# A planned attention and gated-FFN kernel: first transpose in two steps, first weights in halves, burst rules by stage

## The chip, the cores and the metric

The kernel runs on one core of a Trainium2 chip. Its time is the device time of that core in microseconds (us). Six runs of the kernel before are given; the profile comes from one further execution.

## What is computed

Attention with a squared ReLU in place of a softmax, over 8 batches of 12 heads, 448 positions and 64 values a head; then a gated feed-forward network (FFN) over the 3,584 tokens (768 values each, 1,536 inside):

```python
scores = scale * np.matmul(q, k.transpose(0, 1, 3, 2))
attn = np.maximum(scores, 0.0) ** 2 / S
attn_out = np.matmul(attn, v)
x = attn_out.transpose(0, 2, 1, 3).reshape(B * S, H * D)
out = (np.maximum(x @ w_gate, 0.0) * (x @ w_val)) @ w_out
```

## The kernel before

**Work.** The heads are taken in quads: three groups of four heads per batch. A quad goes through these steps. Its queries and keys are brought into a transposed layout `qkT`. A *score step* (`Attention.s`, L622) multiplies four 64x64 corners of the TensorE array at a time and leaves scores in a pair of PSUM banks. A ReLU takes them to SBUF (`at`; ACT at L631 or DVE at L633), a square follows in place (ACT L643 or DVE L645), and a *PV* (`Attention.pv`, L661, 28 matmuls) multiplies by V; its result is copied to `xT` (L676 on ACT). A quad of batches 1 to 7 has seven score steps of four matmuls with 448 columns.

Batch 0 is cut in two so that it can start early: first the 192 query columns (`HALF`) that are loaded first, with all keys, then the 256 late columns. Its quads are transposed on TensorE by `transpose_first` (L494, then L501 for the late queries), those of batch 1 by `transpose_pe` (L527), and all later ones by a copy on DVE (`perm`, L550) and two DMA transposes from the SP queue (L556).

The FFN of batches 0 and 1 is plain (`gv_plain`, L721, twelve blocks of 128 columns, for batch 0 partly with 192 and 256 tokens). The later pairs of batches use a Strassen scheme with seven products (`gv_strassen`, L821), and so does the output product of every pair (`out_both`, L936). Their sums and differences run on DVE.

**Order.** `plan` is a list scheduler that runs while the program is built. Every operation is an `Op` with a cost on each engine that may do it, its inputs, and the buffers that it takes and frees. The planner keeps a clock for each engine, picks the operation that can start first, and emits all operations by their planned start. Each engine then runs its own list in that order; semaphores make it wait where the plan was too early. TensorE has two lists, `att` (attention) and `ffn`. In the opening (`first`) it takes the transposes, batch 0's first scores and its PVs. After that it mixes the lists: `debt` counts FFN time since the last attention step, and when it passes `START` or `LATEST` times the share due, a *burst* of attention steps is taken, up to the next step marked `cut` (`CUTS` says after which steps). Where a gap of TensorE is planned before 21 us (`FILL_UNTIL`), `filler` puts matmuls into it (L1065) that nobody reads; they read a constant tile and write a spare bank.

**Loads.** All loads go out from the POOL queue (L394), in the order of the string `ORDER`: after queries and keys of batch 0, `V` is V of batch 0, `L` its late queries, a digit a weight chunk of 256 columns (gate and value), a letter `abcxyz` a quad of batches 1 and 2, `opqr` the four parts of `w_out`. `raw` has one buffer, so a later quad's load waits for the `perm` of the one before.

```python
    ORDER = 'VL102acbx34y5zroqp'
...
        op = pe(emit, 1.35 if g == 0 else 1.05, deps=st.qk_ops + [id_op], alloc=[ps2, st.qt_buf])
...
    first, att = [list(trans), first, att], []
```

## Time and profile before

| | us |
|---|---|
| median of six runs | 412.49 |
| lowest and highest | 410.02, 415.91 |
| the six | 410.02, 410.5, 415.3, 415.91, 410.35, 414.48 |
| the profiled execution | 409.13 |
| its span | 407.3 |
| matmuls for scores, L622 (756) | 49.9 busy |
| matmuls for PV with `vv`, L661 (700 of 756) | 33.7 busy |
| DMA transposes, issue to landing, median | 6.8 |

The rows name an engine (PE is TensorE's matmuls, PEld its weight loads, DVE VectorE, ACT ScalarE, POOL and SP the two queues that issue DMAs), a line of the kernel, output and input, and how many. "Busy" adds up the durations of single instructions; matmuls overlap each other in the array, so TensorE's busy time has to be read together with what it was busy with. A wait is idle time of an engine just before an instruction, with what ended it. A window such as 60.00:100.00 is a stretch of the span in us.

### The profile page before, as it was taken

Reading aid. Unit: us, or ns where it says so; the run is one execution under the profiler, and the core shown is the slowest. Engines: PE = TensorE matmul, PEld = TensorE weight load, DVE = VectorE, ACT = ScalarE, POOL = GpSimd, SP = SyncE. Lnnn points to the kernel's source line nnn. Section 1 sums busy time; section 2 is a strip of 40 time slices with the busy share of each in tenths; the row PEclk is TensorE's granted clock in tenths of the full one; section 3 lists DMA queues with packets and bytes.
Section 4 is the critical chain, followed back from the end, with each engine's and each line's share of the span. In section 5 each row is a group of like instructions: output and inputs, shape, how many; then the busy total and the mean of one; then the engine's idle time right before and its main releaser. Section 6 shows DMA issues by size and latency. Waiting matters only on the chain.

```text
span 407.3 us, 8787 instructions
## 1 busy us (share of the span) xinstructions
PE 398.3 (98%) x3481; PEld 207.6 (51%) x3481; DVE 324.3 (80%) x573; ACT 257.0 (63%) x385; POOL 74.2 (18%) x119
## 2 busy tenths in 40 slices
PE   8979999999999999999999999999999999999995
PEld 4567654444445544444445544444455555555562
DVE  2777999997899889897798699888798746766652
ACT  2888888556776677888486489756574544434221
POOL 8737215201222112222110122110000000000000
PEclk9999999999999999999999999999999999999999
DMA  8999999988869999885669699750003340000144
GB/s 122 189 199 202 172 177 135 202 123 113 115 89 186 171 167 116 113 94 84 76 78 180 134 183 119 101 69 1 2 0 79 98 98 2 1 0 2 42 106 124
DMA packets 75736, 43.43 MB, mean 107 GB/s; under 512 B 37808, under 2 KB 75696, under 8 KB 75696
## 3 DMA queue, kind: packets, MB, share of 16 engines
q0 software_dynamic: 33328, 23.60, 43.1%
q1 hardware_dynamic: 42208, 19.08, 27.5%
q8 instruction: 27, 0.44, 0.5%
q10 hardware_dynamic: 160, 0.20, 0.1%
q14 instruction: 13, 0.11, 0.1%
HBM read 47.19 MB, written 11.01 MB: 143 GB/s over the span
## 4 chain that ended last, share of the span: by engine, by line
PE 92%; DMA 3%; DVE 3%; ACT 1%; issue 1%; SPq 0%; DVEq 0%
PE ps L821 34%; PE ps L936 23%; PE ps L721 13%; PE ps L622 9%; PE ps L661 8%; PE ps L1065 3%; DMA qkT<-perm 2%; DVE at L633 1%; PE ps L494 1%; DVE at L645 1%; PE ps L527 1%; DMA out_dram<-o 1%; DVE hT L731 0%; SPq L556 0%; ACT xT L676 0%
## 5 line engine op out<-in xcount | busy, mean ns | idle before, releaser
L631 ACT ACTIVATE at<-ps 128x896 bf16<-128x896 f32 (+3 forms) x111 | 97.4, 911 | 20.9 <-PE ps L622 20.7
L770 ACT COPY f<-ps 128x448 f32<-128x448 f32 x99 | 51.8, 532 | 47.0 <-PE ps L821 45.6
L633 DVE TENSOR_SCALAR at<-ps 128x896 bf16<-128x896 f32 (+4 forms) x60 | 63.0, 1052 | 13.3 <-PE ps L622 12.7
L645 DVE TENSOR_TENSOR at<-at 128x896 bf16<-128x896 bf16 (+4 forms) x118 | 69.5, 611 | 3.7 <-ACT at L631 3.3
L821 PE MATMUL ps<-xT,gvT 128*128 128x448 bf16 x216 | 52.6, 353 | 0.0
L643 ACT ACTIVATE at<-at 128x896 bf16<-128x896 bf16 (+4 forms) x53 | 49.8, 940 | 4.1 <-DVE at L633 3.4
L821 PE MATMUL ps<-sx,wv 128*128 128x448 bf16 x216 | 52.2, 353 | 0.0
L821 PE MATMUL ps<-xT,wg 128*128 128x448 bf16 x216 | 51.6, 353 | 0.0
L622 PE MATMUL ps<-qkT 64*64 64x448 bf16 (+2 forms) x756 | 49.9, 341 | 0.5 <-DMA qkT<-perm 0.2
L821 PEld LDWEIGHTS <-gvT 128*128 128x128 bf16 x324 | 30.4, 98 | 32.0 <-issue 5.4
L936 PE MATMUL ps<-wo,hT 128*128 128x384 bf16 x240 | 43.8, 326 | 0.1
L936 PEld LDWEIGHTS <-hT 128*128 128x128 bf16 x312 | 29.7, 98 | 22.9 <-issue 3.9
L394 POOL DMA_DIRECT2D vv<-in_v_dram x44 | 26.7, 620 | 78.1 <-PE ps L622 77.5
L936 PEld LDWEIGHTS <-sh 128*128 128x128 bf16 x288 | 27.0, 98 | 21.3 <-issue 3.7
L772 ACT ACTIVATE f<-ps 128x384 f32<-128x384 f32 x39 | 19.0, 491 | 28.6 <-PE ps L936 28.6
L661 PE MATMUL ps<-at,vv 64*64 64x448 bf16 (+2 forms) x700 | 33.7, 329 | 0.0
L721 PE MATMUL ps<-xT,wv 128*128 128x448 bf16 (+2 forms) x180 | 32.2, 315 | 0.8 <-DVE at L633 0.8
L721 PE MATMUL ps<-xT,wg 128*128 128x448 bf16 (+2 forms) x180 | 32.4, 316 | 0.3 <-ACT xT L676 0.3
L861 DVE TENSOR_TENSOR hT<-ps,g 128x448 bf16<-128x448 f32 x36 | 22.4, 622 | 12.1 <-PE ps L821 12.0
L394 POOL DMA_DIRECT2D raw<-in_k_dram x18 | 11.3, 628 | 112.5 <-DVE perm L550 93.7
L676 ACT CAST xT<-ps 128x896 bf16<-128x896 f32 (+2 forms) x27 | 22.2, 821 | 14.8 <-PE ps L661 13.0
L821 PEld LDWEIGHTS <-wv 128*128 128x128 bf16 x216 | 20.7, 98 | 20.6 <-issue 2.0
(63 smaller groups left out, 484.1 us busy)
## 6 DMA issues: line engine op xcount, KB each, us to landing
out_dram<-o SPq DMA_DIRECT2D x110, 96.0 KB, 2.2
vv<-in_v_dram POOLq DMA_DIRECT2D x44, 112.0 KB, 5.5
raw<-in_k_dram POOLq DMA_DIRECT2D x18, 224.0 KB, 4.9
raw<-in_q_dram POOLq DMA_DIRECT2D x18, 224.0 KB, 6.8
wg<-in_moe_w_gate_dram POOLq DMA_DIRECT2D x6, 384.0 KB, 8.9
wv<-in_moe_w_val_dram POOLq DMA_DIRECT2D x6, 384.0 KB, 10.3
wo<-in_moe_w_out_dram POOLq DMA_DIRECT2D x4, 576.0 KB, 11.9
gvT<-in_k_dram POOLq DMA_DIRECT2D x6, 224.0 KB, 5.8
```

What stands on the lines that cost most here:

```text
L394: op = Op({"POOL": (0.5 + 0.0004 * n_desc,) * 2}, lambda: nc.gpsimd.dma_start(out=dst(), in_=src), deps=deps, alloc=alloc)
L622: nc.tensor.matmul(banks()[64 * j:64 * j + 64, z, h2], lhsT=self.k_of(j, h2, k), rhs=self.q_of(j, h2), start=True, stop=True)
L631: nc.scalar.activation(self.at_of(i, m), banks(), AF.Relu)
L633: nc.vector.tensor_scalar_max(self.at_of(i, m), banks(), 0.0)
L643: nc.scalar.activation(a, a, AF.Square)
L645: nc.vector.tensor_tensor(a, a, a, ALU.mult)
L661: nc.tensor.matmul(ps[64 * h2:64 * h2 + 64, ps2.idx + j, :n], lhsT=st.v_of(j, h2, c), rhs=self.at_of(c)[64 * j:64 * j + 64, 0, h2], start= ...
L721: nc.tensor.matmul(ps[:, pb.idx, :n], lhsT=w[:, kd, fc], rhs=xT_t[xbuf[b].idx][:, kd, cols], start=(kd == 0), stop=(kd == KD - 1))
L770: nc.scalar.copy(dst, src)
L821: nc.tensor.matmul(ps[:, pb.idx, :S], lhsT=w(g)[:, fc], rhs=rhs, start=start and g == 0, stop=stop and g == KH - 1, skip_group_check=True)
L861: h0 = Op({"DVE": V448}, lambda pb=prev["A"], gb=prev["g0b"], mf=prev["mf"]: nc.vector.tensor_tensor(h_slot(b, mf), ps[:, pb.idx, :S], g_t ...
L936: nc.tensor.matmul(ps[:, pb.idx, :OH], lhsT=lhs(kf), rhs=rhs(kf), start=start and kf == 0, stop=kf == FH - 1, skip_group_check=True)
```

## The change

It does five things. (1) The first quad of batch 0 is transposed in two steps: first the slots whose queries and keys are needed first, then the remaining keys into another bank pair, with a copy of their own (`late_keys`); score steps on early keys need only the first. (2) The order of loads changes: late queries before V, weight chunk 1 first, then chunk 0 in two halves of 128 columns (`6` is columns 128 to 255, `0` then columns 0 to 127), quads of batch 1 in their natural order, the parts of `w_out` spread. (3) The constants of the burst rule become pairs, chosen by `late`, which is 1 once the FFN's next work is that of batches 2 and 3 or later (segment 3); the cut marks and the places of PV and of the transposes change. (4) In the opening the next attention step of the other list (late queries) may be taken where it would end before any of the first steps could start (`SPARE`); and an attention step may be put between the two products of an FFN block where it fits in the wait (`APART`). Squares and the sums for the output product start later in the comparison by `YIELD`. (5) The planner's model changes: POOL starts at 1.25 us, and DMA transposes queue differently.

In the diff, lines that are left out are marked by "..."; the marks `kind` on operations, which only give them names, are left out too.

```diff
self.load = self.land = 0.0
-        self.xbar = self.cut = False
...
+        self.cut = False
+        self.xbar = 0
         self.start = self.end = self.eng = None
...
     MARGIN = 4.0
-    LATE = 3.0
+    LATE = (3.0, 3.0)
     RESERVE = (1000.0, 12.0, 2.0)
...
     FILL_MARGIN = 0.1
-    WINDOW = 5
-    ATT_WINDOW = 2
-    START = 0.8
-    LATEST = 3.0
-    HOLD = 0.1
-    SLACK = 0.1
-    CUTS = ((1, 3), (0, 1, 3, 5, 6), (2, 6), (2, 6))
+    WINDOW = (5, 3)
+    ATT_WINDOW = (3, 1)
+    START = (0.7, 0.5)
+    LATEST = (1.8, 3.0)
+    HOLD = (0.1, 0.4)
+    SLACK = (0.2, 0.1)
+    CUTS = ((1, 3), (1, 5, 6), (2, 4, 6), (2, 6))
     GV_ORDER = '1256734'
...
     BUFFERS = (3, 11, 3, 5, 4, 5, 3)
-    PV_AT_0 = 1
+    URGENT = {'sh': -0.5, 'perm': 0.5}
+    YIELD = {'sq': 0.1, 'sh': 0.1}
+    SPARE = -0.3
+    APART = (0.5, 0.5)
+    PV_AT_0 = 0
     QT = 3
     PART = 6
-    PV_AT = 1
-    T_AT = 3
+    PV_AT = (1, 1)
+    T_AT = (1, 0)
     MORE_UNTIL = 4
     BY_PE = 6
-    ORDER = 'VL102acbx34y5zroqp'
+    ORDER = 'LV160ab2c3x4oy5rzqp'
...
         self.banks = banks
-        self.t = {}
+        self.t = {"POOL": 1.25}
         self.ops = []
...
             if d.eng != "PE" or "PE" not in op.engs:
-                r = max(r, d.end + (self.LATE if d.xbar else 0.0))
+                r = max(r, d.end + (self.LATE[d.xbar - 1] if d.xbar else 0.0))
         for b in op.alloc:
...
         if op.xbar:
-            self.dmaq = max(self.dmaq, s) + 1.5
-            op.end = max(op.end, min(self.dmaq + 2.0, s + 13.0))
+            queued = self.dmaq > s + 2.1
+            op.end = max(op.end, min(self.dmaq + 10.0, s + 14.0)) if queued else op.end
+            self.dmaq = max(self.dmaq, s) + (4.5 if queued else 2.5)
         for b in op.alloc:
...
             b.readers -= 1
-            b.last = max(b.last, op.end + (self.LATE if op.land else 0.0))
+            b.last = max(b.last, op.end + (self.LATE[1] if op.land else 0.0))
             if b.readers == 0:
...
-    def fits(ops, now):
+    def fits(ops, now, late):
...
         for o, t in zip(ops, times):
-            if t > now + P.SLACK:
+            if t > now + P.SLACK[late]:
                 return False
...
         cands = []
+        late = int(not ffn or ffn[0][1] >= 3)
         for op in active:
...
             if b is not None:
-                cands.append((b[0], b[2], 1, b[1], op))
+                cands.append((b[0] + P.YIELD.get(op.kind, 0.0), b[2] - P.URGENT.get(op.kind, 0.0), 1, b[1], op, b[0]))
         if pi < len(pool):
...
                     cands.append((b[0], b[2], 3, "PE", x[0]))
+            b = P.best(att[0]) if P.SPARE is not None and att else None
+            if b is not None:
+                s = b[0] + att[0].engs["PE"][0] + P.SPARE
+                if all(c[2] != 3 or s <= c[0] for c in cands):
+                    cands.append((b[0], b[2], 4, "PE", att[0]))
         else:
             A = F = None
-            for i, op in enumerate(att[:P.ATT_WINDOW]):
+            for i, op in enumerate(att[:P.ATT_WINDOW[late]]):
                 b = P.best(op)
...
                     A = (*b, i)
-            for i, (op, _) in enumerate(ffn[:P.WINDOW]):
+            for i, (op, _) in enumerate(ffn[:P.WINDOW[late]]):
                 b = P.best(op)
...
                 pick = "F" if F is not None else None
+                if F is not None and A is not None and A[0] + att[A[3]].engs["PE"][0] + P.APART[late] <= F[0]:
+                    pick = "A"
             elif A is not None and F is not None:
...
                 if inside:
-                    pick = "A" if A[0] <= max(F[0], now + P.HOLD) else "F"
+                    pick = "A" if A[0] <= max(F[0], now + P.HOLD[late]) else "F"
                 else:
                     n = next((i for i, o in enumerate(att) if o.cut), len(att) - 1) + 1
-                    if debt >= P.LATEST * n * share:
+                    if debt >= P.LATEST[late] * n * share:
                         pick = "A" if A[0] <= F[0] + 0.15 else "F"
-                    elif debt >= P.START * n * share and A[0] <= now + 0.15 and fits(att[:n], now):
+                    elif debt >= P.START[late] * n * share and A[0] <= now + 0.15 and fits(att[:n], now, late):
                         pick = "A"
...
         assert cands, f"no operation can start: {ai} {len(ffn)} {len(active)} {pi}"
-        s, _, kind, e, op = min(cands, key=lambda c: c[:3])
+        c = min(cands, key=lambda c: c[:3])
+        s, _, kind, e, op = c[:5]
+        if kind == 1:
+            s = c[5]
         if e == "PE" and s < P.FILL_UNTIL:
...
             first = [x[1:] if x and x[0] is op else x for x in first]
+        elif kind == 4:
+            ai += 1
+            del att[0]
         elif pick == "A":
...
-    def load_gv(c):
-        cols = slice(c * WC, (c + 1) * WC)
+    def load_gv(m0, m1):
+        cols = slice(m0 * 128, m1 * 128)
         for ops, sb, w in ((wg_op, wg, moe_w_gate), (wv_op, wv, moe_w_val)):
             src = w.rearrange("(kd p) f -> p kd f", p=128)
-            ops[c] = dma_in(lambda sb=sb: sb[:, :, cols], src[:, :, cols], 768,
-                            2.15 if wv_op or sb is wv else 2.8)
+            op = dma_in(lambda sb=sb: sb[:, :, cols], src[:, :, cols], 768,
+                        1.075 * (m1 - m0) + (0.0 if wv_op or sb is wv else 0.65))
+            for m in range(m0, m1):
+                ops[m] = op
...
         st = quads[(0, g)]
         st.qt_buf = Buf(r_qt)
-        ps2, ps2b = bank2(MORE_PAIRS), bank2(FIRST_PAIRS)
-        n1 = (NT + QT) * P2
...
-        def emit():
+        ps2, ps2k, ps2b = bank2(MORE_PAIRS), bank2(FIRST_PAIRS), bank2(FIRST_PAIRS)
+        n0, n1 = 2 * HALF, (NT + QT) * P2
+        two = g == 0
+        def emit_slots(pair, slots, shift=0):
             for j in range(2):
-                for t in range(NT):
+                for t in slots:
                     p0, c0, n = (0, 2 * t * P2, 128) if t < QT else (64, (QT + t) * P2, 64)
                     for h2 in range(2):
-                        nc.tensor.transpose(ps_b[64 * h2:64 * h2 + 64, ps2.idx + j, c0:c0 + n],
+                        nc.tensor.transpose(ps_b[64 * h2:64 * h2 + 64, pair.idx + j, c0 - shift:c0 - shift + n],
                                             st.raw()[p0:128, 2 * j + h2, t, :], ident[p0:128, p0:128])
...
-        op = pe(emit, 1.35 if g == 0 else 1.05, deps=st.qk_ops + [id_op], alloc=[ps2, st.qt_buf])
-        cps = [copy_qk(op, ps2, lambda j=j: first_cols(st, j, j + 1, 0, n1),
-                       lambda j=j: ps_b[:, ps2.idx + j:ps2.idx + j + 1, :n1], ((0.45, 0.57), (0.62, 0.77))) for j in range(2)]
+        def copies(op, us, c1):
+            return [copy_qk(op, ps2, lambda j=j: first_cols(st, j, j + 1, 0, c1),
+                            lambda j=j: ps_b[:, ps2.idx + j:ps2.idx + j + 1, :c1], us) for j in range(2)]
+        if two:
+            op = pe(lambda: emit_slots(ps2, range(QT)), 0.7, deps=st.qk_ops + [id_op], alloc=[ps2, st.qt_buf])
+            opk = pe(lambda: emit_slots(ps2k, range(QT, NT), n0), 0.6, deps=[op], alloc=[ps2k])
+            cps = copies(op, ((0.30, 0.42), (0.40, 0.55)), n0)
+            st.late_keys = [copy_qk(opk, ps2k, lambda: first_cols(st, 0, 2, n0, n1),
+                                    lambda: ps_b[:, ps2k.idx:ps2k.idx + 2, :n1 - n0], ((0.37, 0.5), (0.51, 0.66)))]
+            ops = [op, opk]
+        else:
+            op = pe(lambda: emit_slots(ps2, range(NT)), 1.05, deps=st.qk_ops + [id_op], alloc=[ps2, st.qt_buf])
+            cps = copies(op, ((0.45, 0.57), (0.62, 0.77)), n1)
+            st.late_keys = []
+            ops = [op]
         st.qt_ops = {0: cps}
...
                          lambda: ps_b[:, ps2b.idx:ps2b.idx + 2, :2 * S - n1], ((0.37, 0.5), (0.51, 0.66)))
-            st.qt_ops[HALF] = cps + [cp]
+            st.qt_ops[HALF] = cps + st.late_keys + [cp]
             return op
-        return op, rest
+        return ops, rest
...
         op = Op({"SP": (2.6, 2.6)}, emit, deps=[perm], alloc=[st.qt_buf], reads=[pb])
-        op.land = 7.4 if b == 2 else 5.4
-        op.xbar = True
+        op.land = 5.4
+        op.xbar = 1 if b == 2 else 2
         st.qt_ops = {0: [op]}
...
-            op = pe(emit, mm_time(m, n) + 0.01, deps=self.st.qt_ops[self.c0], alloc=[ps2, at], reads=[self.st.qt_buf],
+            keys = self.st.late_keys if self.b == 0 and self.c0 == 0 and slots[-1] >= QT else []
+            op = pe(emit, mm_time(m, n) + 0.01, deps=self.st.qt_ops[self.c0] + keys, alloc=[ps2, at], reads=[self.st.qt_buf],
                     mode="64x64")
...
-                op = pe(emit, mm_time(KD, n), deps=x_ops + [w_op[mf * 128 // WC]], alloc=[pb], reads=[xbuf[b]], grp=(b, mf, c0))
+                op = pe(emit, mm_time(KD, n), deps=x_ops + [w_op[mf]], alloc=[pb], reads=[xbuf[b]], grp=(b, mf, c0))
                 ffn.append((op, seg))
...
              load_out(*out_of[x])
+        elif x == "6":
+            load_gv(1, 2)
+        elif x == "0" and "6" in Planner.ORDER:
+            load_gv(0, 1)
         else:
-            load_gv(int(x))
+            load_gv(2 * int(x), 2 * int(x) + 2)
     for b in range(3, B):
...
         PV(n)
-    first, att = [list(trans), first, att], []
+    first, att = [sum(trans, []), first, att], []
...
             att.append(A_[n].s(i))
-            if i == (Planner.PV_AT if n >= 2 * NQ else Planner.PV_AT_0) and n not in (NQ, 2 * NQ):
+            sd = A_[n].b >= 3
+            if i == (Planner.PV_AT[sd] if n >= 2 * NQ else Planner.PV_AT_0) and n not in (NQ, 2 * NQ):
                 PV(n - 1)
-            if i == Planner.T_AT and n >= 2 * NQ - 1:
+            if i == Planner.T_AT[sd] and n >= 2 * NQ - 1:
                 T(n + 1 - NQ)
...
                 att[-1].cut = True
```

## The prediction

> **What bounds the kernel now.** I read the busy rows of the page first, then TensorE's instructions in order of time, then VectorE's in the opening, then the busy time by stage.
>
> The page's busy rows (engines' totals, then two of the rows in 40 slices):
>
> ```profile
> PE 398.3 (98%) x3481; PEld 207.6 (51%) x3481; DVE 324.3 (80%) x573; ACT 257.0 (63%) x385; POOL 74.2 (18%) x119
> ...
> PE   8979999999999999999999999999999999999995
> ...
> DVE  2777999997899889897798699888798746766652
> ```
>
> TensorE is the bound, but its busy time holds the fillers of L1065, whose results nobody reads. The timeline of TensorE shows them (start, us taken, line, count, and in brackets what it waited for):
>
> ```profile
> 1.39 4.20 PE L1065 MATMUL ps<-woT 128*128 128x437 bf16 x11 [1.39 <-DVE woT L1052]
> 5.72 1.69 PE L494 MATMUL ps<-ident,gvT 128*64 128x128 bf16 x28
> 7.34 1.92 PE L1065 MATMUL ps<-woT 128*128 128x417 bf16 x5
> 9.20 1.17 PE L622 MATMUL ps<-qkT 64*64 64x192 bf16 x24
> 10.30 0.98 PE L1065 MATMUL ps<-woT 128*128 128x374 bf16 x4
> ...
> 27.14 0.66 PE L721 MATMUL ps<-xT,wv 128*128 128x192 bf16 x6 [0.75 <-DVE at L633]
> ...
> 37.13 0.76 PE L622 MATMUL ps<-qkT 64*64 64x448 bf16 x12
> ```
>
> After the first transposes (5.72) the ten later filler groups take 6.1 us from start to next start, and the waits between 23 and 32 us are 0.57, 0.53, 0.75 and 0.27 = 2.1. So 8.2 us before 37.13, the first score step of batch 1, is unproductive. After 37 us the timeline names one wait of TensorE, 0.19 us at 151.58. What the change can win therefore lies in the opening; later it can only keep or lose.
>
> VectorE in the opening:
>
> ```profile
> 7.46 0.49 DVE L471 COPY qkT<-ps 128x640 bf16<-128x640 bf16 x1 [4.31 <-PE ps L494]
> 10.18 0.96 DVE L633 TENSOR_SCALAR at<-ps 128x768 bf16<-128x768 f32 x1 [2.23 <-PE ps L622]
> ...
> 22.33 1.82 DVE L633 TENSOR_SCALAR at<-ps 128x1024 bf16<-128x1024 f32 x2 [3.25 <-PE ps L622]
> ...
> 33.09 1.02 DVE L645 TENSOR_TENSOR at<-at 128x1024 bf16<-128x1024 bf16 x2
> ```
>
> It ends the last square of batch 0 at 34.1. On the way it waits 2.23 us (scores held up behind fillers) and 3.25 us (scores of the late queries not yet made). By stage (busy us of PE, PEld, DVE, ACT, POOL; clock; DMA; GB/s):
>
> ```profile
> 18.00:26.00 8.00, 6.71 (x188) 5.37 (x188) 4.75 (x9) 6.56 (x12) 2.42 (x4) 1.00 1.46 197
> ...
> 60.00:100.00 40.00, 40.00 (x328) 19.32 (x329) 37.38 (x52) 26.09 (x37) 10.68 (x16) 1.00 1.01 147
> 100.00:150.00 50.00, 49.80 (x435) 25.16 (x433) 44.99 (x81) 36.65 (x53) 9.76 (x16) 1.00 0.98 136
> ```
>
> TensorE is full from 60 us on, with VectorE close behind at 93% and 90%.
>
> **The change part by part.** The instruction orders of the two programs have the same matmuls except fillers: 37 become 23. The rest is moved.
>
> *First filler and first transposes.* The opening filler grows from 11 of 437 columns to 15 of 420. In the trace 11 start 0.364 us apart, all 11 alike over 4.0 us: 437 columns at half the rate of the FFN later (24 of 448 columns in 4.65 us), though the profile's clock row says 1.00. At that rate 15 take 15 x 0.35 = 5.25, ending at 1.39 + 5.25 = 6.64; the data were there at 5.72. Cost 0.92 us. The Trainium skill ("TensorE: Matmul & The Clock Gate", section "What's actually happening") says the array starts at half rate and is released after about 3.4 us of sustained work, in a window that runs free; by that the last five would run at full rate and end near 5.8, a cost of 0.1. The trace had no release within 4.0 us, and the five fillers at 7.34 again start 0.37 apart, so I take 6.64 and keep 0.8 us as upside.
>
> *First quad in two steps.* 12 transposes at 1.69/28 = 0.060 each end at 7.4, and the two 384-column copies start at 7.5 (ACT and DVE, one each). The 16 key transposes (0.96) end at 8.3, eight score matmuls follow with no filler between, and the first ReLU starts at 8.6 to 8.7. Before, it was 9.78 on ACT and 10.18 on DVE. The extra copy of late keys (ACT, 0.59 by the 512-column row) lies in ACT's wait.
>
> *Late queries first, and allowed into gaps.* Their three loads (128 KB each) go ahead of V on the POOL queue, so V lands about 384 KB / 190 GB/s = 2 us later, near 16; its first reader, the PV that began at 18.10, comes no earlier than 16 after. Queue POOL carries two DMAs more, at 0.88 us each, while it waits anyway. Scores of the 256 late columns now stand in the order among those of the first 192, so the 3.25 us wait should go. What sets the end of batch 0's attention then is the vector engines' work. By the changed order, DVE does up to its last square there: 4 ReLUs of 768 columns (3.8 us by 0.96), 4 of 1024 (4.7), one each of 384 and 512 (1.2), 7 squares of 768 (3.4 by 0.49), 8 of 1024 (5.0 by 0.63), one of 512 (0.4), 2 copies of 640 (1.0), three other copies (1.4), 2 products of 192 (0.7): 21.7 us. ACT by the same kind of count has 21.6. Both are full. From 7.5: 7.5 + 21.7 = 29.2, plus 0.9 of waiting for the first scores, plus small waits. Before, those were 0.44 + 0.36 + 0.25 = 1.05; with more scores at hand I take half, 0.5. So the last square ends at 30.6, against 34.1. The last PV (0.9) follows it directly, and the first score step of batch 1 starts near 31.6. Before that step the changed order has done 36 FFN matmuls of 192 columns where before had 72; 36 x 0.092 (12 take 1.10 in the chain) = 3.3 us is still to be paid. The comparable point of before is 37.13 - 3.3 = 33.8. **Gain 33.8 - 31.6 = 2.2 us**, the 0.92 already in it.
>
> *Weight chunk in halves, new load order.* The first FFN block needs columns 0 to 127, now the last half to land, after 3.55 MB. By the GB/s rows that is 22.3 us at the old rate. Rows of a half are 256 bytes. On this queue the trace's packet records have a median of 60 ns at 512 bytes and 51 at 384; the line through them gives 42 at 256, so four halves take 84/60 of two wholes (2.0 us each): +1.6, landing near 25. TensorE gets there at 25 to 26. Taken: 0. The skill ("DMA: Bandwidth & Descriptors", section "Specifications") speaks against the halves: below 512 bytes a transfer is read, changed and written again. Were a half as dear as a whole, landing would be near 27.5, and the FFN, transposes and first of the last two PVs queued behind it in TensorE's order would finish near 32.5, past the last square: 1.5 us lost. The 384-byte packets in the trace show no such step, so I take the trace.
>
> *Burst rules, cuts, YIELD, URGENT, DMA-transpose model.* These only reorder. TensorE changes between 64-row and 128-row work 184 times instead of 180. In the chain eight score matmuls take 0.50 and twelve 0.69, so entering costs 0.12; six FFN matmuls take 1.24 and nine 1.81, so 0.10 back. 4 x 0.1 = **0.4 us lost**. 15 squares of 896 columns go from DVE to ACT (15 x 0.61 = 9.2 us off), four ReLUs come back (4.2 us): hidden behind TensorE as long as its work is ready. The DMA transposes of batch 2 are first read after 8 us more of other work than before, so the 0.19 us wait can go; worth 0 to 0.2, taken 0. SP's stores shift against transposes by at most three pairs; the stores have five output buffers and 2.2 us of landing. Taken 0.
>
> **Sum.** 409.13 (the profiled execution: span 407.3 and 1.8 around it) - 2.2 + 0.4 = 407.3. The median of the six runs is 412.49, 1.0082 of it: 407.3 x 1.0082 = **410.7**. Bounds of this case: no small waits (-0.5), filler by the skill (-0.8), no cost per switch (-0.4) give 405.6, scaled 408.9; twice the small waits and the dear halves give 409.3, scaled 412.7.
>
> **The rivals.**
> - *A larger gain.* Of the 8.2 unproductive us, all but 1.05 (2,528 filler columns at full rate) and the late start (0.92) go: 6.2 us, 402.9, scaled 406.2. For it: the planner finds little to fill. Against it: 21.7 us of vector work cannot end before 29.2. A gain over 1% needs the quick filler and hardly a wait besides. 0.20.
> - *The change does not do it.* Later V, dear halves or the vector engines waiting for each other turn the removed fillers into plain idle time: gain 0 to 0.3, 409.3 with the switches, scaled 412.7. For it: before had 2.1 us of such waits from 23 to 32 besides its fillers. 0.14.
> - *Slower: VectorE falls behind in 60 to 200 us.* FFN is put ahead of batch 2's attention by 8 us, so the same 11 quads must fit in about 130 us instead of 138. A quad takes DVE some 6 us; 11 of them are 67 us, so its load there rises from 90% by about 3 points, less the 5 us moved to ACT (4 points). Where bursts crowd, the average does not help: in the stretch from the 300th to the 900th FFN matmul there are 46 bursts instead of 40, more of them of three steps, which fill all three PSUM pairs, and whatever TensorE has next that needs a bank waits for a ReLU (1.05 us). At 0.16 us each, 46 bursts cost 7.4: 414.7, scaled 418. It turns the forecast gain into a loss at 0.04 us a burst and into over 1% at 0.13. Against it: before ran the same kind of mix with 0.19 us of waits. 0.16.
>
> **How the numbers follow.** The main case has 0.50. The range takes it whole, the second rival, and most of the first; the runs of before themselves lie between 410 and 416. **406 to 415**; left out are the slow rival and the tip of the first. About 1% is what a measurement of this kernel can tell from no change: 4.1 us. Faster by more: the first rival and a corner of the main case, 0.23. Slower by more: 0.16 and nearly nothing else, 0.17. Within: 0.60.
>
> **What would show it.** The first transposes near 6.6 (5.8 if the array's rate rises earlier); VectorE's first ReLU near 8.7; no wait above 1 us on DVE between 9 and 30; its last square of batch 0 near 30.6; first 448-column score near 31.6; filler groups after the first of under 1.5 us in all. Right on later stages: TensorE's waits after 40 us below 0.5 us in all. Wrong: waits of TensorE on ReLUs (DVE or ACT) between 100 and 200 us, on the first weights near 25, or on a DMA transpose. A last square before 29.5 would mean that I costed the vector work too dear.

## The result and the profile after

| | us |
|---|---|
| before, median of 64 runs | 412.41 (408.26 to 418.92) |
| after, median of 29 runs | 408.95 (407.53 to 411.55) |
| ratio after to before | 0.9939, 95% interval 0.9922 to 0.9956 |
| the profiled execution after | 408.44, span 406.6 |

The changed kernel is 0.6% faster (0.4 to 0.8%), inside the 1% that was counted as no change. The ratio leaves out the runs that lie more than 1.5% above the fastest of their kernel (15 of the 64 of before, none of the 29 after), so it stands for about 2.5 us, while the medians of all runs differ by 3.5. The two profiled executions differ by 0.7 us only, 409.13 against 408.44. And the runs of the changed kernel lie within 4 us, those of before within 11. These two facts are what the experiments had to explain.

The page of the changed kernel, engine totals and two of the rows in 40 slices:

```profile
PE 395.1 (97%) x3467; PEld 205.2 (50%) x3467; DVE 321.9 (79%) x562; ACT 263.8 (65%) x397; POOL 75.6 (19%) x121
...
PE   8789999999999999999999999999999999999995
...
DVE  3998945998788888999799689888698846766552
```

TensorE is still the bound. It is busy 3.2 us less, with 14 fillers fewer; VectorE's first slices are fuller, as more of batch 0's attention is done there by 18 us.

TensorE in order of time (start, us taken, line, count, wait):

```profile
1.39 4.69 PE L1117 MATMUL ps<-woT 128*128 128x420 bf16 x15 [1.39 <-DVE woT L1104]
6.01 0.89 PE L521 MATMUL ps<-ident,gvT 128*64 128x128 bf16 x28
6.94 0.41 PE L663 MATMUL ps<-qkT 64*64 64x192 bf16 x8
...
25.34 0.66 PE L766 MATMUL ps<-xT,wg 128*128 128x192 bf16 x6 [0.50 <-DVE at L676]
...
30.86 0.55 PE L663 MATMUL ps<-qkT 64*64 64x448 bf16 x8
...
92.27 0.57 PE L663 MATMUL ps<-qkT 64*64 64x448 bf16 x8 [0.74 <-DMA qkT<-perm]
```

Transposes start at 6.01 and take 0.89 us for 28, where they took 1.69. The first FFN block waits for a ReLU of VectorE, not for weights. The first score step of batch 1 comes at 30.86. The one wait of any size after 40 us is on a DMA transpose.

VectorE in order of time:

```profile
8.49 0.96 DVE L676 TENSOR_SCALAR at<-ps 128x768 bf16<-128x768 f32 x1 [1.55 <-PE ps L663]
...
21.73 1.22 DVE L676 TENSOR_SCALAR at<-ps 128x1024 bf16<-128x1024 f32 x1 [0.37 <-PE ps L663]
...
28.67 0.68 DVE L688 TENSOR_TENSOR at<-at 128x1024 bf16<-128x1024 bf16 x1
```

The 3.25 us wait for scores of the late queries is gone (between 9 and 29 us two waits are left, 0.41 and 0.37), and the last square of batch 0 ends at 29.3 instead of 34.1.

By stage (busy us of PE, PEld, DVE, ACT, POOL; clock; DMA; GB/s):

```profile
18.00:26.00 8.00, 5.69 (x165) 4.48 (x162) 7.63 (x12) 7.17 (x11) 3.45 (x7) 1.00 1.60 191
60.00:100.00 40.00, 39.26 (x303) 18.53 (x300) 33.30 (x47) 27.86 (x39) 9.00 (x14) 1.00 1.23 146
100.00:150.00 50.00, 49.74 (x430) 24.00 (x427) 42.18 (x77) 37.35 (x53) 9.74 (x16) 1.00 0.87 143
```

VectorE works 7.63 of 8 us in the opening (4.75 before) and only 33.3 of 40 us from 60 us on (37.38 before): no engine but TensorE came near its limit there.

**Where the time came from and went.** To compare programs that do the same work in another order, I take the start of a step and subtract the useful matmul time that stands before it in the program. Each matmul has a fixed price, its distance to the next one in a long uninterrupted group (0.191 us for an FFN matmul of 448 columns, 0.053 for a score, 0.1625 for an output matmul, and so on; 375.2 us in all). The rest is *unproductive time*: fillers, waits, mode switches (TensorE going from 64-row to 128-row work or back), matmuls at half rate. The table gives it before the first score step of batch 1, before batch 2's third and batch 4's second quad, and at the last matmul.

| profiled execution | batch 1 | batch 2, third quad | batch 4, second quad | end | its time | median of runs |
|---|---|---|---|---|---|---|
| before | 14.1 | 15.8 | 19.3 | 27.0 | 409.13 | 412.41 |
| after | 11.1 | 14.2 | 18.8 | 26.4 | 408.44 | 408.95 |
| opening only | 12.5 | 17.8 | 21.0 | 29.0 | 411.01 | 410.75 |
| rules only | 14.6 | 19.4 | 24.8 | 33.5 | 415.82 | 415.19 |
| short filler | 11.4 | 14.0 | 18.6 | 26.2 | 408.46 | 410.37 |
| late queries not in gaps | 11.6 | 18.0 | 22.1 | 30.6 | 412.71 | 412.32 |
| before, long filler | 13.3 | 19.7 | 24.9 | 32.6 | 414.68 | 413.27 |
| opening only, last weights early | 10.7 | 16.6 | 22.3 | 31.3 | 413.74 | 413.72 |
| one step | 11.9 | 17.0 | 21.9 | 29.9 | 412.09 | 411.22 |
| burst rules back | 10.4 | 15.4 | 20.0 | 28.8 | 410.87 | 412.05 |
| before, w_out spread | 12.5 | 15.5 | 18.6 | 27.7 | 409.74 | 409.24 |
| after, w_out bunched | 11.0 | 15.1 | 21.2 | 30.0 | 412.59 | 413.25 |
| whole chunk | 11.0 | 14.0 | 18.6 | 26.1 | 408.37 | 409.36 |
| attention window | 10.7 | 16.6 | 21.6 | 30.2 | 412.46 | 411.54 |

The first two rows: the opening gains 3.0 us, and 2.4 of them are given back by 160 us, 0.74 of it by the wait at 92.27. So in these two executions the change is worth 0.6 us at the last matmul. Yet the medians differ by 3.5: the profile of before is that of a lucky execution (3 of the 64 runs of before are as fast as 409.13).

### The profile page after: what moved, and what is told of

Same layout as the page of the kernel before. It is cut to its first block, busy times and chain, and to the rows that moved or that the text cites. A ratio compares the mean times of both kernels' runs of the same rounds, so it can differ in the third digit from the quotient of the medians.

```text
span 406.6 us, 8761 instructions
## 1 busy us (share of the span) xinstructions
PE 395.1 (97%) x3467; PEld 205.2 (50%) x3467; DVE 321.9 (79%) x562; ACT 263.8 (65%) x397; POOL 75.6 (19%) x121
## 4 chain that ended last, share of the span: by engine, by line
PE 84%; DMA 9%; POOL 3%; ACT 1%; issue 1%; DVE 0%; SPq 0%; DVEq 0%; ACTq 0%; POOLq 0%
PE ps L872 36%; PE ps L987 24%; PE ps L766 10%; PE ps L663 8%; PE ps L705 7%; DMA gvT<-in_q_dram 5%; DMA qkT<-perm 3%; DMA gvT<-in_k_dram 1%; ACT at L674 1%; POOL gvT L415 1%; POOL wv L415 1%; POOL wg L415 1%; DMA out_dram<-o 1%; POOL vv L415 0%; PE ps L567 0%
## 5 line engine op out<-in xcount | busy, mean ns | idle before, releaser
L674 ACT ACTIVATE at<-ps 128x896 bf16<-128x896 f32 (+3 forms) x107 | 93.2, 908 | 15.3 <-PE ps L663 14.8
L819 ACT COPY f<-ps 128x448 f32<-128x448 f32 x101 | 53.4, 533 | 48.3 <-PE ps L872 45.5
L676 DVE TENSOR_SCALAR at<-ps 128x896 bf16<-128x896 f32 (+3 forms) x64 | 68.5, 1073 | 13.2 <-PE ps L663 11.3
L686 ACT ACTIVATE at<-at 128x896 bf16<-128x896 bf16 (+3 forms) x71 | 64.4, 928 | 1.7 <-DVE at L676 1.3
L688 DVE TENSOR_TENSOR at<-at 128x896 bf16<-128x896 bf16 (+2 forms) x100 | 59.3, 618 | 2.4 <-ACT at L674 2.1
L663 PE MATMUL ps<-qkT 64*64 64x448 bf16 (+2 forms) x756 | 50.8, 338 | 3.1 <-DVE qkT L496 0.7
L987 PEld LDWEIGHTS <-hT 128*128 128x128 bf16 x312 | 29.5, 98 | 22.8 <-issue 4.0
L987 PEld LDWEIGHTS <-sh 128*128 128x128 bf16 x288 | 27.1, 98 | 21.6 <-issue 4.3
L720 ACT CAST xT<-ps 128x896 bf16<-128x896 f32 (+2 forms) x26 | 21.8, 837 | 19.3 <-PE ps L705 18.8
L821 ACT ACTIVATE f<-ps 128x384 f32<-128x384 f32 x37 | 18.1, 489 | 24.7 <-PE ps L987 22.4
L663 PEld LDWEIGHTS <-qkT 64*64 64x64 bf16 x756 | 18.0, 105 | 29.2 <-issue 24.9
L977 DVE SCALAR_TENSOR_TENSOR o<-ps,f 128x384 f32<-128x384 f32 x40 | 22.2, 555 | 12.7 <-PE ps L987 10.8
## 6 DMA issues: line engine op xcount, KB each, us to landing
wo<-in_moe_w_out_dram POOLq DMA_DIRECT2D x4, 576.0 KB, 12.5
```

The source lines that it names most:

```text
L663: nc.tensor.matmul(banks()[64 * j:64 * j + 64, z, h2], lhsT=self.k_of(j, h2, k), rhs=self.q_of(j, h2), start=True, stop=True)
L674: nc.scalar.activation(self.at_of(i, m), banks(), AF.Relu)
L676: nc.vector.tensor_scalar_max(self.at_of(i, m), banks(), 0.0)
L686: nc.scalar.activation(a, a, AF.Square)
L688: nc.vector.tensor_tensor(a, a, a, ALU.mult)
L819: nc.scalar.copy(dst, src)
```

## The experiments

Each group of four experiments has its own runs of the kernel before, on another chip of the same kind: their median is 411.33 (35 runs) for the first four, 412.00 (35) for the next four, 411.83 (33) for the last four. Ratios are to those, with 95% intervals. In the cuts of code, "..." marks lines that are left out.

### 1 and 2: the two halves of the change alone

*Opening only* takes the changed kernel and puts the later part back, that is the constants of the bursts and cuts, `YIELD`, `URGENT`, `APART`, the places of PVs and transposes, and the model of DMA transposes:

```diff
-    ATT_WINDOW = (3, 1)
...
-    LATEST = (1.8, 3.0)
...
+    ATT_WINDOW = (2, 2)
...
+    LATEST = (3.0, 3.0)
...
-    YIELD = {'sq': 0.1, 'sh': 0.1}
+    YIELD = {}
```

> The changed kernel with its later part undone: burst constants, cut marks, YIELD, URGENT, APART, PV and transpose places and the model of DMA transposes as before; the opening (two steps, load order, halves, late queries in gaps, POOL clock) as changed. Theory A (the gain is made in the opening, and the burst rules give back about 2 us between 84 and 160 us): first 448-column score near 31 us, and faster than the change, ratio to before about 0.989 to 0.992 (170 switches instead of 184 are worth some 1.4 us). Theory B (the opening's gain is lost later anyway, and what makes the median fall is that the new rules keep DMA transposes from coming late): ratio 0.998 to 1.002, with runs spread as widely as before's.

410.75 us, ratio 0.9992 (0.9969 to 1.0015): no gain that can be told. TensorE has waits that neither kernel has (and one of 0.65 us on a ReLU at 55.46):

```profile
65.63 1.31 PE L765 MATMUL ps<-xT,wg 128*128 128x448 bf16 x6 [0.93 <-DMA wg<-in_moe_w_gate_dram]
67.47 1.31 PE L765 MATMUL ps<-xT,wv 128*128 128x448 bf16 x6 [0.53 <-DMA wv<-in_moe_w_val_dram]
```

These are the last weight chunk's, which stands behind quad `y` and now behind one part of `w_out` too. With the old rules TensorE comes to it sooner than it lands.

*Rules only* undoes the opening and keeps the later part:

```diff
-    SPARE = -0.3
+    SPARE = None
...
-    ORDER = 'LV160ab2c3x4oy5rzqp'
+    ORDER = 'VL102acbx34y5zroqp'
...
-        self.t = {"POOL": 1.25}
+        self.t = {}
...
-        two = g == 0
+        two = False
...
```

> The changed kernel with its opening undone: one-step transpose, load order of before, no late queries in gaps, POOL clock of before; burst rules and model as changed. Theory A: the opening's waits and fillers are back, first 448-column score near 37 us of comparable work, 198 switches instead of 180: ratio 1.003 to 1.008. Theory B: ratio 0.993 to 0.996, and a spread as narrow as the change's.

415.19 us, ratio 1.0094 (1.0068 to 1.0120): the rules alone lose 0.9%. So neither half carries a gain by itself, and the two cannot be added up: each half is planned together with the loads and the opening. Note that this program has the old load order; its VectorE shows, in order of time:

```profile
91.09 1.36 DVE L809 TENSOR_TENSOR woT<-wo 128x2304 bf16<-128x2304 bf16 x1 [2.06 <-DMA wo<-in_moe_w_out_dram]
```

### 3: the changed kernel with the short first filler

```diff
+        n = min(n, 11) if cold else n
```

> The changed kernel with 11 instead of 15 matmuls in its first filler group and nothing else. Theory A (the array's rate rises after about 4.0 us of filler, so that the longer filler pays for itself in transposes at 0.03 us instead of 0.06): with 11 the first transposes start near 5.7 but take about 1.7 us instead of 0.9, and the next filler group runs at half rate; the first score step of quad 0 comes no earlier than 7.0, total within 0.5 us of the change. Theory B (the filler only delays): the transposes start at 5.7 and the first score comes 0.3 us earlier or more, total 0.3 us less.

410.37 us, ratio 0.9984 (0.9954 to 1.0013). TensorE at the start:

```profile
1.39 4.03 PE L1118 MATMUL ps<-woT 128*128 128x420 bf16 x11 [1.39 <-DVE woT L1104]
5.89 1.07 PE L521 MATMUL ps<-ident,gvT 128*64 128x128 bf16 x28 [0.46 <-DMA gvT<-in_q_dram]
6.99 0.41 PE L663 MATMUL ps<-qkT 64*64 64x192 bf16 x8
```

Transposes start 0.12 us sooner and run slower (1.07 instead of 0.89), so the first scores come at 6.99 instead of 6.94. In this execution the four more fillers cost nothing and save nothing; from there both profiles are alike to the end (26.2 against 26.4). The medians, 1.4 us apart, come from different sets of runs, and the intervals of the two ratios just touch (0.9954 and 0.9956). Whether the long filler makes a run surer to start fast stays open.

### 4: late queries not allowed into gaps

```diff
-    SPARE = -0.3
+    SPARE = None
```

> The changed kernel with SPARE off: late queries may not go into the opening's gaps; all else as changed. Theory A (late-query scores in the gaps are what removes VectorE's wait of 3.25 us): the wait is back (2 us or more on DVE before the first 1024-column ReLU), fillers return (15,367 columns instead of 8,828), first 448-column score 3 us later for its work, ratio 0.999 to 1.003. Theory B (the two-step transpose and the load order do most of it): ratio stays at 0.994 to 0.996.

412.32 us, ratio 1.0027 (1.0009 to 1.0045): the gain is gone. The first score step of batch 1 still starts early, but with part of batch 0 undone behind it; VectorE waits again for scores of the late queries, 2.45 us at 20.20. From batch 1's first to second quad unproductive time grows from 11.6 to 14.6 us (after: 11.1 to 11.5), then a DMA transpose is late (TensorE, in order of time):

```profile
33.01 0.38 PE L663 MATMUL ps<-qkT 64*64 64x448 bf16 x4 [0.54 <-ACT at L674]
...
39.44 0.66 PE L766 MATMUL ps<-xT,wv 128*128 128x192 bf16 x6 [0.67 <-DVE hT L776]
...
93.81 0.57 PE L663 MATMUL ps<-qkT 64*64 64x448 bf16 x8 [1.55 <-DMA qkT<-perm]
```

So the early scores of the late queries are the part of the opening that pays, about 3 us by the second quad in these two plans.

### 5: the kernel before with the long first filler

```diff
+        n = n + 4 if n == 11 else n
```

> The kernel before, with 15 instead of 11 matmuls in its first filler group and nothing else. Theory A (with 11 it is chance whether the array's full rate is granted near 6 us or only near 9 to 10, since a gap before the transposes breaks the busy stretch; 15 in a row reach it always, and this is why the runs of before spread over 10 us): the five fillers after the transposes take about 1.1 us and not 1.9, the runs spread over no more than 5 us, and the ratio is 0.994 to 0.998. Theory B (the rate at the start doesn't matter to the whole): ratio 1.000 to 1.003, spread as before.

413.27 us (408.08 to 416.97), ratio 0.9997 (0.9959 to 1.0036): no difference that can be told, and the runs spread over 9 us, so the filler does not narrow them. The profiled execution is a long one, 414.68 us, and shows what the lucky profile of before did not. VectorE in order of time:

```profile
83.79 0.62 DVE L731 TENSOR_TENSOR hT<-ps,g 128x448 bf16<-128x448 f32 x1
88.31 1.36 DVE L761 TENSOR_TENSOR woT<-wo 128x2304 bf16<-128x2304 bf16 x1 [3.90 <-DMA wo<-in_moe_w_out_dram]
89.71 1.36 DVE L761 TENSOR_TENSOR woT<-wo,woT 128x2304 bf16<-128x2304 bf16 x1
90.98 0.62 DVE L731 TENSOR_TENSOR hT<-ps,g 128x448 bf16<-128x448 f32 x1
```

and TensorE of the same execution:

```profile
87.28 1.30 PE L721 MATMUL ps<-xT,wv 128*128 128x448 bf16 x6
91.65 1.62 PE L721 MATMUL ps<-xT,wg 128*128 128x448 bf16 x6 [3.08 <-DVE hT L731]
93.06 2.45 PE L721 MATMUL ps<-xT,wv 128*128 128x448 bf16 x6
```

The first sum on `w_out` waits 3.90 us for its load. The next FFN product (90.98) stands behind it on VectorE's list; TensorE needs the PSUM bank that this product frees and waits 3.08 us. After this idle stretch TensorE falls back to half rate: five more matmuls start 0.19 us apart, those from 92.7 to 94.9 start 0.37 apart (the group at 93.06 takes 2.45 us, the one at 87.28 took 1.30), and the clock row reads 0.51 from 92.5 to 96. That costs some 1.6 us more, so the late load cost this execution about 4.7 of the 5.6 us by which it is longer than the profile of before. It is the only one of the fourteen profiles in which TensorE is seen to stand still for `w_out`.

The four loads of `w_out` had been issued together. The view of the tile `wo`, issue to landing, for the kernel before:

```profile
L394 POOL DMA_DIRECT2D wo<-in_moe_w_out_dram x4: 843/853/862, 65.7 to 68.2; - x4
DMA to landing us min/median/max: 8.8/11.9/16.4
```

and for this execution:

```profile
L394 POOL DMA_DIRECT2D wo<-in_moe_w_out_dram x4: 843/853/862, 64.9 to 67.4; - x4
DMA to landing us min/median/max: 11.2/14.6/20.8
```

The last landed at 68.2 + 16.4 = 84.6 in the profile of before, and the sum that needs it started at 85.09: a margin of 0.5 us. Here it landed at 67.4 + 20.8 = 88.2, which is when the sum started. In the changed kernel the string `ORDER` has the four parts at three places, one behind chunk 4, one behind chunk 5, and the last two together behind quad `z`:

```profile
L415 POOL DMA_DIRECT2D wo<-in_moe_w_out_dram x4: 835/882/909, 42.9 to 70.5; - x4
DMA to landing us min/median/max: 11.1/12.5/13.7
```

The last one, issued at 70.5, lands 13.2 us later at 83.7, and the sum starts at 86.34, a margin of 2.7 us. From here on the theory was: the changed kernel's lower median and narrower spread come, to a good part, from `w_out` no longer being loaded in a bunch.

### 6: opening only, with the last weight chunk ahead of quad y

```diff
-    ORDER = 'LV160ab2c3x4oy5rzqp'
+    ORDER = 'LV160ab2c3x45oyrzqp'
```

> The kernel of the opening-only run, with the last weight chunk loaded ahead of quad y instead of behind it. Theory A (with the old burst rules the opening's gain was lost because TensorE came to the last chunk before it had landed: 0.93 + 0.53 us of named waits on it near 66 us and idle around it): the wait is gone, the overhead of TensorE at the first score step of batch 2's second quad falls from 14.9 to 13.2 or less, ratio 0.993 to 0.996. Theory B (old rules lose it to the vector engines): the wait goes, but the ratio stays above 0.997.

413.72 us, ratio 1.0024 (0.9990 to 1.0057). The waits near 66 us are gone and others have come: 1.70 us on a weight chunk at 36.96, 1.29 on a DMA transpose at 67.57, 1.28 and 0.83 on ReLUs at 148 to 150. Taking away one wait of the opening-only kernel does not make it fast; the planner's list is rebuilt each time, and the loads share one queue.

### 7: the first quad transposed in one step

```diff
-        two = g == 0
+        two = False
```

> The changed kernel with its first quad transposed in one step again. Theory A (two steps save the fillers before the first scores, about 1 us at the first ReLU, of which the full vector engines pass on most): first ReLU near 9.5 instead of 7.4, first 448-column score about 1 us later, ratio 0.996 to 0.998. Theory B (by then the second quad's data set the pace): first ReLU later, but the first 448-column score within 0.3 us of 30.9, ratio 0.993 to 0.995.

411.22 us, ratio 0.9997 (0.9965 to 1.0028). The first ReLU starts at 8.99 (7.43 in the changed kernel), but batch 1's first score step at 30.51, as early as ever. Of the 1.56 us at the first ReLU some 0.5 are not the step's: the first filler ended at 6.60 instead of 6.08, because in this execution it ran at half rate almost to its end. At batch 1's first score step 0.8 us of unproductive time are left (11.9 against 11.1). At the end it is 3.5 us, with new waits on the way: 0.54 us on weights at 67.06, 0.80 and 0.45 on DMA transposes, 0.63 and 0.25 on VectorE. So two steps are not what brings batch 1 forward; the run cannot say what they are worth in an otherwise equal plan.

### 8: seven constants of the bursts as before

```diff
-    START = (0.7, 0.5)
-    LATEST = (1.8, 3.0)
...
-    CUTS = ((1, 3), (1, 5, 6), (2, 4, 6), (2, 6))
...
+    START = (0.8, 0.8)
+    LATEST = (3.0, 3.0)
...
+    CUTS = ((1, 3), (0, 1, 3, 5, 6), (2, 6), (2, 6))
```

> The changed kernel with the burst constants and cut marks of before (windows, START, LATEST, HOLD, SLACK, CUTS); YIELD, URGENT, APART, the places of PV and transposes and the model of DMA transposes as changed. Theory A (what the new order of loads needs from the later part are YIELD and the DMA model, which set when quad loads and DMA transposes are wanted; the burst constants hardly matter): ratio 0.993 to 0.997. Theory B (the separate burst rules carry it): ratio above 0.998, with waits on weights or on DMA transposes of 1 us and more.

The two windows, `HOLD` and `SLACK` go back as well. 412.05 us, ratio 0.9999 (0.9967 to 1.0031). The least unproductive time of all at batch 1 (10.4), and then TensorE, in order of time:

```profile
63.02 1.31 PE L766 MATMUL ps<-xT,wg 128*128 128x448 bf16 x6 [0.84 <-DMA wg<-in_moe_w_gate_dram]
64.81 1.31 PE L766 MATMUL ps<-xT,wv 128*128 128x448 bf16 x6 [0.48 <-DMA wv<-in_moe_w_val_dram]
...
141.34 0.57 PE L663 MATMUL ps<-qkT 64*64 64x448 bf16 x8 [1.36 <-DMA qkT<-perm]
```

With the old constants TensorE comes to the FFN's last chunk and to batch 4's attention before their data have landed. The changed kernel has neither wait, so what its burst constants do there is to fit the work to the new order of loads; that this is all they do is not shown.

### 9: the kernel before, with only w_out spread

```diff
-    ORDER = 'VL102acbx34y5zroqp'
+    ORDER = 'VL102acbx34oy5rzqp'
```

> The kernel before, with one edit: the loads of w_out are spread between the loads of batch 2's quads, in the order that the changed kernel has (o, y, 5, r, z, q, p), instead of four in a row behind quad z. The opening is left as it was. Theory A (part of the changed kernel's advantage is that w_out lands without a bunch; in the kernel before the sums on w_out start within 1 us of their last load, and where the load is late VectorE's queue stands and TensorE with it, 3 us in the one execution that showed it): no wait of VectorE on wo, the spread of the runs narrows to under 5 us, and the median falls by 1 to 2 us, to about 410.5; first 448-column score step stays near 37. Rival B (the spread of before comes from the chip or from the opening's clock, not from w_out): median 411.5 to 413 and runs over 8 us or more, as before.

409.24 us (11 of 12 runs between 408.36 and 411.13, one at 414.69), ratio 0.9924 (0.9896 to 0.9951). Theory A gave 410.5; the fall is larger, 2.6 us. This one edit of the string is worth as much as the whole change (0.9939); the two ratios, 0.15% apart, cannot be told from each other. There is no wait of VectorE on `wo`:

```profile
L394 POOL DMA_DIRECT2D wo<-in_moe_w_out_dram x4: 823/860/894, 41.6 to 67.9; - x4
...
DMA to landing us min/median/max: 12.2/14.7/16.3
```

The last two, issued from 67.0 on, took 12.2 and 14.3 us. The profile itself (409.74) is not better than that of before, 409.13: it has a wait of 1.29 us on a DMA transpose at 62.07 and ends with 27.7 us of unproductive time against 27.0. Its margin at `w_out` is not wide either: the last part landed at 82.2 and the sum started at 83.16, 1.0 us later, against 0.5 in the profile of before. What fell is not the best time but the usual one. Of 103 runs of before that went with these experiments, the middle half lies between 410.8 and 412.6, and only 17 are below 410.5; here 10 of 12 are. The best of those 103, 407.38, is as low as the best of the changed kernel, 407.53.

### 10: the changed kernel, with w_out in a bunch

```diff
-    ORDER = 'LV160ab2c3x4oy5rzqp'
+    ORDER = 'LV160ab2c3x4y5zroqp'
```

> The changed kernel, with one edit: the four loads of w_out are issued in one bunch behind quad z, as in the kernel before. The opening is untouched, so the first 448-column score step stays near 30.9. Theory A (w_out in a bunch lands at the moment when VectorE needs it): VectorE waits on wo (over 0.5 us) near 85 to 90 in the profile or in part of the runs, the median rises by 1 to 3 us to 410 to 412, and the runs spread over more than the 4 us of the changed kernel. Rival B: no wait on wo, median within 0.8 us of 409, spread unchanged.

413.25 us (411.29 to 415.04), ratio 1.0027 (0.9999 to 1.0056). Everything else of the change is in it, its opening too (30.75), and nothing of the gain is left; it is more than theory A's 1 to 3 us worse than the changed kernel's 408.95. The spread is no wider, 3.8 us, against what theory A said. VectorE in order of time:

```profile
89.15 1.36 DVE L809 TENSOR_TENSOR woT<-wo 128x2304 bf16<-128x2304 bf16 x1 [2.15 <-DMA wo<-in_moe_w_out_dram]
```

and TensorE:

```profile
76.05 0.57 PE L663 MATMUL ps<-qkT 64*64 64x448 bf16 x8 [1.58 <-DMA qkT<-perm]
...
146.59 0.38 PE L663 MATMUL ps<-qkT 64*64 64x448 bf16 x4 [0.88 <-ACT at L674]
148.21 0.38 PE L663 MATMUL ps<-qkT 64*64 64x448 bf16 x4 [0.25 <-ACT at L674]
```

VectorE waits for `w_out`, as expected, but TensorE shows no wait right behind it. Against the changed kernel it loses 0.9 us up to batch 2's third quad (its waits for DMA transposes there are 1.58 us against 0.74; the late one was issued at 65.0, just ahead of the four loads, and took 11.0 us to land), 1.5 more up to batch 4's second quad, and 1.2 more to the end. The wait on `w_out` itself is thus only part of it; how much of the rest is the bunch on the DMA engines and how much is the re-planned order, this run does not separate. Nor does experiment 9, where the quads' loads move with the parts of `w_out` and the order is planned anew.

Over all profiles: of the four programs with a bunch, three show VectorE waiting for `w_out` (2.06, 3.90 and 2.15 us; the last load took 20.4 to 20.8 us to land there, 16.4 in the one without a wait). Of the ten with the loads spread, none does.

### 11: the first weight chunk whole

```diff
-    ORDER = 'LV160ab2c3x4oy5rzqp'
+    ORDER = 'LV10ab2c3x4oy5rzqp'
```

> The changed kernel with the first weight chunk loaded whole again (512-byte rows, two transfers instead of four); the order of the instructions on the engines is otherwise the same. My step (the halves cost nothing and save nothing, TensorE comes to the first FFN block at 25 to 26 anyway): first FFN matmuls at 25.3 as before or up to 0.5 later, median within 1 us of 409. Rival (the halves are what lets the FFN start on time): the first FFN matmuls wait 1 us or more on wg or wv near 25, last score of batch 0 and first 448-column score later by as much, 410 to 411. Second rival (halves are dear by their 256-byte rows): the whole chunk lands earlier and the time falls by up to 1.5 us.

409.36 us (407.95 to 410.18), ratio 0.9926 (0.9893 to 0.9958). TensorE in order of time:

```profile
25.21 0.66 PE L766 MATMUL ps<-xT,wg 128*128 128x192 bf16 x6 [0.20 <-DVE at L676]
...
30.73 0.55 PE L663 MATMUL ps<-qkT 64*64 64x448 bf16 x8
```

The order of work is the changed kernel's, and so are the starts: 25.21 against 25.34, 30.73 against 30.86. Halves or whole, the first FFN block waits for VectorE. The halves do land later: the last of them at 25.69, the whole chunk at 24.38, with packets of 256 bytes that took 41 ns (median) where those of 512 took 60. Their reader starts at 25.83, so the 1.3 us are hidden, but by 0.14 us only. Loading in halves is worth nothing here, and costs nothing in the time.

### 12: fewer mode switches

```diff
-    ATT_WINDOW = (3, 1)
+    ATT_WINDOW = (2, 2)
```

> The changed kernel with the choice of attention steps for the first batches limited to 2 (later ones 2) as before, instead of 3 and 1. The plan has 180 mode switches instead of 184, the opening's fillers are the same. Theory (the switches are what is given back after 84 us, 0.1 us each): 0.4 us less, 408.5, no new wait. Rival (each edit re-plans the whole, and new waits on DMA transposes or ReLUs of 0.5 to 1.5 us appear after 60 us): 409.5 to 411.5 in spite of fewer switches.

411.54 us, ratio 0.9994 (0.9961 to 1.0028), with 180 mode switches instead of 184. The rival's case: TensorE waits 1.68 and 0.56 us on the last weight chunk at 64 to 66 us, 0.61 on a DMA transpose at 141.75, 0.89 and 0.43 on ReLUs near 148. The price of a switch cannot be read under such waits; it stays an estimate. No program tried is measurably better than the changed kernel; the kernel before with `w_out` spread and the changed kernel with a whole chunk equal it.

## Why the prediction was right, and where it was not

The forecast was 410.7 us with a range of 406 to 415; 408.95 lies in it, and a change within 1% was the likeliest class. Its steps stand differently, and that the number came so near is in part luck.

*The first filler.* Predicted to end at 6.64 at half rate throughout, with 5.8 by the Trainium skill's rule ("TensorE: Matmul & The Clock Gate", section "What's actually happening"). In the trace the first eleven intervals between these matmuls are 0.32 to 0.35 us and the last three 0.18: the rate rose some 3.8 us after the first matmul, and the transposes started at 6.01. The rule came nearer in this execution. In another profiled opening of the same form all fourteen intervals were 0.33 to 0.35 us, as I had it (opening only). The fillers after the first took 1.8 us from start to next start, where I had said under 1.5.

*Scores and ReLUs.* The first ReLU of all was predicted at 8.6 to 8.7 and came at 7.43, on ScalarE, because the transposes ran at full rate; VectorE's first, predicted at 8.7, came at 8.49. The last square of batch 0 was predicted to end at 30.6 and ended at 29.3; batch 1's first score step was predicted at 31.6 and started at 30.86. The mechanism held: VectorE is nearly full from 8.5 us on. Counted from 7.5 us, as in the forecast, it waited 1.0 us for its first scores (0.9 predicted) and 0.8 us later on (0.5 predicted). The text had said that an end before 29.5 would mean vector work costed too dear, and it was so: to the end of that square it was busy 20.1 us, not the 21.7 counted. Its instructions overlap by some 0.07 us each (the ReLU at 8.49 takes 0.96, and the square behind it starts at 9.37), which the count had left out in part. The gain of the opening is 3.0 us between these two profiles, where I had 2.2. By the long-filler and the spread runs, whose opening is that of before with its moment of full rate elsewhere, before itself stands at 12.5 to 14.1 us of unproductive time there, so that the opening is worth 1.4 to 3.0. No run shows this gain in a median by itself.

*Halves at nothing.* Right in the time, shown by experiment 11. The landing was predicted near 25, 1.6 us later than the whole chunk; it was 25.69, 1.3 us later. The packets of 256 bytes took 41 ns, against 42 from the line through the larger ones, so there is no step below 512 bytes. But the reader came only 0.14 us behind the landing.

*Late queries.* Right in place, and in size as far as one other plan can show it: without them in the gaps VectorE's wait is back, and some 3 us with it (experiment 4).

*Later stages.* Predicted loss 0.4 us for switches, and waits below 0.5 in all. Measured: 2.4 us given back by the end, 0.74 us of it the DMA transpose that I had costed at 0 (a gain of up to 0.2 in my text). A wait on a DMA transpose was one of the signs that I had named for being wrong. The remaining 1.7 us are named by no wait in the timeline; part may be the switches and shorter bursts, which experiment 12 could not show. Against the profile of before the term was mis-sized, 0.4 for 2.4. But that profile is the odd one: from batch 1's first score step to the end it collects 12.9 us of unproductive time, the changed kernel 15.3, and before with `w_out` spread 15.2. Against this last one nothing is given back, so the 2.4 may be the luck of one execution and not a cost of the new rules. The rival of an overrun VectorE did not come about: it has more room from 60 to 150 us, not less. Related waits on ReLUs near 148 do appear in other plans (experiments 6, 10, 12).

*The scaling to the median.* This is the step that failed. I took the ratio of before's median to its profile, 1.0082, as common to all executions and carried it over: 407.3 became 410.7, 3.3 us more. For the changed kernel the ratio is 408.95 / 408.44 = 1.0012, 0.5 us. Such a ratio belongs in part to the one execution that was profiled: in the table the median lies between 1.4 us below the profile (before with the long filler) and 3.3 us above it (before), and 1.9 us above it for the short filler, whose `w_out` is spread. In part it belonged to the old order of the loads, which my text had looked at for the first weight chunk and for V alone. I never costed the move of `w_out` out of its bunch, though the diff shows it in the same string. Experiments 9 and 10 show that this edit of the order makes the difference in the median, in both directions: 2.6 us are won by it in one kernel, some 4 lost by undoing it in the other.

So the errors partly cancel: the profile was predicted 1.1 us too low (0.8 too little gained in the opening, 2.0 too little given back, 0.1 of rounding), and the scaling put on 2.8 us too much; together the forecast was 1.7 us too high.

What stays open is the way from the order of the loads to the median. No profile of the unchanged kernel before was caught in one of its usual, longer executions. That VectorE's wait on `w_out` is what those executions have is argued, not shown: it rests on one long execution of the long-filler program, which differs from before by four matmuls ahead of 7 us, and on the medians of experiments 9 and 10. What that execution shows does not reach the usual case. A stretch of 3.4 us at half rate lowers the mean granted clock of a run by 0.004, and the profiles without such a stretch have 0.997 to 1.000. Of the 103 runs of before, 26 stand at 0.996 or less, with a median of 413.98; the other 77 have 411.39, still 2.3 us above the profile. And such runs are as frequent in the changed kernel, 7 of 29. Nor does the mean say where the stretch was: the short filler's profile has one in the opening (20.0 to 23.4), where it cost at most 0.3 us.

## What to carry to other kernels

A profile shows one execution: before adding a margin to its time, ask which of its loads landed only just in time, because a load that lands 0.5 us before its reader in one profile was a wait of 3.9 us in the profile of nearly the same program, and an engine that runs its list in order passes it on. Try to spread loads that are issued in a bunch, and look at landing times (the last part of `w_out` took 16 to 21 us in a bunch, 11 to 15 when spread), not only at named waits. When a scheduler builds the order, the parts of a change cannot be priced one by one: undoing either half, or one constant, moved waits of 0.5 to 2 us between weights, DMA transposes and ReLUs.

## What the hardware showed that was not expected

TensorE's rise from half to full rate is not at a fixed time. With a continuous first filler (15 matmuls of 420 columns, 437 in the long filler) it came 3.2 to 4.9 us after the first matmul in eight profiles, and in two (opening only; before with the long filler) not within the filler's 5.4 to 5.7 us. With 11 matmuls and a pause, the same code gave this in the kernel before with `w_out` spread (TensorE, in order of time), where the second filler took 1.92 us in the profile of before:

```profile
5.67 1.13 PE L494 MATMUL ps<-ident,gvT 128*64 128x128 bf16 x28
6.73 1.06 PE L1065 MATMUL ps<-woT 128*128 128x417 bf16 x5
```

The clock row says full speed in both, also where the matmuls run at half rate. The start of batch 1 differs by 1.6 us between these two profiles (35.54 against 37.13).

TensorE can also fall back. After the idle stretch of 3.08 us in the long-filler run it worked at half rate for 3.4 us, and there the clock row showed it (0.51). After waits of 1.2 to 1.8 us, in eight other profiles, no such stretch followed. In the short filler's profile it came at 20.0 us, where no single wait ahead of it is longer than 0.81 us (clock row 0.50).

Four loads of 576 KB issued within 2.5 us took 8.8 to 20.8 us to land, each behind the last, and the longest landing differed between profiles of nearly the same load order from 16.4 to 20.8 us.
